# The first chunk's output product in seven half-size products, with its weights' sums a slot earlier

## The chip, the cores and the metric

The kernel runs on one core of one Trainium2 chip. The metric is the device time of one launch in microseconds, the median of three runs. The profile is one execution of the same program, with the engines' instructions, their waits and the transfers recorded: PE is TensorE, DVE VectorE, ACT ScalarE, POOL GpSimd, SP SyncE, which here only starts transfers.

## What is computed

Two layers stand behind one another. The first is an attention over channels, the second a gated feed-forward layer on its result:

```python
qn = q / (norm(q, axis=1) + 1e-6)          # q, k, v: 4 x 6016 x 256
kn = k / (norm(k, axis=1) + 1e-6)
a = softmax(kn.transpose(0, 2, 1) @ qn / tau)   # 256 x 256 for each batch entry
x = (v @ a).reshape(24064, 256)
gate = sigmoid(x @ w_gate)                 # w_gate, w_val: 256 x 1536
out = (gate * (x @ w_val)) @ w_out         # w_out: 1536 x 256
```

The kernel never forms x. It multiplies the 256 x 256 attention weights of a batch entry into w_gate and w_val once, which gives G and H, and then feeds v to these.

## The kernel before

**Tiling.** A batch entry b has 6016 rows, that is 47 tiles of 128. They are worked on in 12 chunks `(b, ci)` of four tiles (512 rows), the last one of three. The hidden width of 1536 is cut into 12 blocks of 128, f = 0 to 11. One pass of the innermost loop, for one f of one chunk, is called a slot here, and slots of a batch entry are counted as 12 ci + f: slot 10 is f = 10 of the first chunk, slot 12 is f = 0 of the second.

**A slot.** `glu(b, ci, f)` runs two matmuls of 128 x 512 into `ps_gate` (weights `gh_G`), ScalarE takes their tanh into `g_sb` (L647), then PE gets what the caller has put in between, then two matmuls of 128 x 512 into `ps_val` (weights `gh_H`), and VectorE joins the two into block f of `hT` (L650). `ps_gate` and `ps_val` have two PSUM buffers each, so the gate matmuls of slot n wait for the tanh of slot n - 2, and the val matmuls of slot n wait for the VectorE instruction of slot n - 2.

**What stands in between.** The output product of chunk n is worked off during chunk n + 1: `out_work` makes a list of matmuls, and `run_work` takes a twelfth of it between the gate and the val matmuls of each slot. Before the change there are two forms of this list:

- The first chunk, `(0, 0)`, is `plain`: for each of its four row tiles 12 matmuls of 128 x 256 (`single`, L754), 48 in all, four in a slot. Each reads a block of `hT` as its stationary operand and a row block of `w_out_sb`. ScalarE copies each finished tile to `out_sb` (L760).
- Every other chunk takes its tiles in two pairs p = 0, 1, and the product of a pair as a 2 x 2 block product (rows by hidden blocks by output columns) in seven half-size products instead of eight: `PRODUCTS` names them, `ORDER` gives their order. Each consists of six matmuls of 128 x 128, so there are 84 matmuls, seven in a slot. The operands are blocks of `hT` and of `w_out_sb`, or sums of such blocks. The sums of `hT` blocks are made on VectorE by `a_sum` (L676, L678, L680: three instructions for the first half of the hidden blocks, at f = 7, 9, 11 of the chunk itself, and three for the second half, at f = 0, 2, 4 of the next chunk). The sums of `w_out` blocks, `w_sums`, are made once. When z1 is done, ScalarE copies three of the four regions to `m_sb` and GpSimd adds in it twice (`part`); when v2 is done, ScalarE copies the PSUM bank to `out_sb` and GpSimd adds twice (`whole`).

**The weights' sums.** `w_out` comes as three float32 tiles `w_f32[0..2]`, each with the rows of four hidden blocks. GpSimd casts them into `w_out_sb` (`copy_w_out`, slot 8), and makes five sums m = 0 to 4, each in three instructions, one for each tile (`sum_w_out`, L228), at the slots 11 (m = 1), 13 (m = 0), 15 (m = 3), 17 (m = 2) and 19 (m = 4). The last one needs the other sign, so there each instruction is followed by a multiplication by -1, on GpSimd too (L230). The products use them as follows: y1 takes sum 1, x1 sum 0, z1 sum 3, z2 sum 2, v2 sum 4; x2 and y2 take `w_out_sb` itself.

**What sets the order.** The order of the instructions on each engine is written out by hand: `side_work` hangs other work on slots, and within a slot the loop first calls `glu`, then puts `a_sum`, then the work hung on that slot. No scheduler moves anything. GpSimd's queue also issues most loads: `load_qk` of the next batch entry at slot 9 (four transfers), `load_v` at slot 10 of the first chunk and at the first slot of the following ones.

The lines of one slot in the main loop that the change touches, with the two tables it uses:

```python
NEXT_SLOTS = {0: 0, 2: 1, 4: 2}
OWN_SLOTS = {7: 0, 9: 1, 11: 2}
...
                    if f in next_sums and prev != (0, 0):
                        a_sum(*prev, 1, next_sums[f])
                if f in OWN_SLOTS and not final and (b, ci) != (0, 0):
                    a_sum(b, ci, 0, OWN_SLOTS[f])
                for fn, a in spill.get((b, ci, f), []) + side.get((ci, f), []):
                    fn(*a)
```

Of the kernel before, what the change touches and what calls it, by code (L numbers as in the profile page):

```python
# [12 lines left out]
ACT = mybir.ActivationFunctionType  # L13
ALU = mybir.AluOpType
# [37 lines left out]
OWN_SLOTS = {7: 0, 9: 1, 11: 2}  # L52
# [3 lines left out]
def kernel(  # L56
# [20 lines left out]
    nc = tc.nc  # L77
# [10 lines left out]
    FC = DFF // P  # L88
# [41 lines left out]
    def mm(out, lhsT, rhs, start, stop, **kw):  # L130
        nc.tensor.matmul(out, lhsT=lhsT, rhs=rhs, start=start, stop=stop, **kw)  # L131
# [30 lines left out]
    t0, nt = groups0[0]  # L162
# [39 lines left out]
    for f0, nf in pieces:  # L202
        if f0 + nf == DFF:
            load_v(0, 1)
        for w, src in enumerate((moe_w_gate, moe_w_val)):
            nc.gpsimd.dma_start(
                out=w_sb[w][f0 // FG][:, :, ds(f0 % FG, nf)],
                in_=src.rearrange("(t p) f -> p t f", p=P)[:, :, ds(f0, nf)],
# [5 lines left out]
    for n in range(FC // TPC):  # L214
        w_f32[n] = f32pool.tile([P, TPC, C], FP32, tag="f32", name="w_f32")
        nc.gpsimd.dma_start(
            out=w_f32[n], in_=moe_w_out.rearrange("(t p) c -> p t c", p=P)[:, n * TPC : (n + 1) * TPC, :]
# [5 lines left out]
    def sum_w_out(m, n):  # L223
        (k0, c0), op, (k1, c1) = B_SUMS[m]
        w = w_f32[n]
        out = w_sums[:, m, n * 2 : (n + 1) * 2, :]
        in0, in1 = w[:, k0::2, ds(c0 * P, P)], w[:, k1::2, ds(c1 * P, P)]
        nc.gpsimd.tensor_tensor(out=out, in0=in0, in1=in1, op=op)  # L228
        if m == 4:
            nc.gpsimd.tensor_scalar(out=out, in0=out, scalar1=-1.0, scalar2=None, op0=ALU.mult)  # L230


    st = {}
# [449 lines left out]
    stores = []  # L683

    def out_tile(b, ci):
        if (b, ci) not in ffn:
            ffn[b, ci] = opool.tile([P, TPC, C], FP32, tag="osb", name="out_sb")
        return ffn[b, ci]

    def out_work(b, ci):  # L690

        nt = groups[ci][1]
        half = nt // 2
        hT = hts[b, ci]
        work = []
        states = [{} for _ in range(half)]
        singles = {}
        plain = (b, ci) == (0, 0)

        def product(p, name, i):  # L700
            state = states[p]
            region, a, w = PRODUCTS[name]
            first = name == "y1" and i == 0
            if first:
                state["ps"] = pso.tile([P, CH], FP32, tag="o", name="ps_o")
            g, j = divmod(i, FC // 4)
            if isinstance(a, tuple):
                lhsT = hT[:, 2 * i + a[1], ds((a[0] * half + p) * P, P)]
            else:
                lhsT = sums[b, ci, g][:, a, j, ds(p * P, P)]  # L710
            rhs = w_out_sb[:, 2 * i + w[0], ds(w[1] * P, P)] if isinstance(w, tuple) else w_sums[:, w, i, :]
            mm(
                state["ps"][:, ds(region * P, P)],
                lhsT,
                rhs,
                start=first,
                stop=(i == FC // 2 - 1),
                skip_group_check=True,
            )
            if i == FC // 2 - 1:  # L720
                if name == "z1":
                    part(p)
                elif name == "v2":
                    whole(p)

        def part(p):

            m = states[p]["m"] = mpool.tile([P, 3, P], FP32, tag="m", name="m_sb")
            nc.scalar.copy(m, states[p]["ps"][:, : 3 * P].rearrange("p (n c) -> p n c", c=P))  # L729
            nc.gpsimd.tensor_tensor(out=m[:, 1, :], in0=m[:, 1, :], in1=m[:, 2, :], op=ALU.add)  # L730
            nc.gpsimd.tensor_tensor(out=m[:, 2, :], in0=m[:, 1, :], in1=m[:, 0, :], op=ALU.add)  # L731

        def whole(p):

            o = out_tile(b, ci)
            nc.scalar.copy(  # L736
                o[:, p : p + half + 1 : half, :],
                states[p]["ps"].rearrange("p (t c) -> p t c", c=C),
            )
            blocks = o.rearrange("p t (h c) -> p (t h) c", c=P)  # L740
            c00, c11 = 2 * p, 2 * (half + p) + 1
            ends = blocks[:, c00 : c11 + 1 : c11 - c00, :]
            mids = blocks[:, c00 + 1 : c11 : max(1, c11 - c00 - 2), :]
            last = (b, ci) == (B - 1, NCH - 2)
            add = nc.gpsimd.tensor_tensor
            add(out=ends, in0=ends, in1=states[p]["m"][:, 1:3, :], op=ALU.add)  # L746
            add(out=ends, in0=ends, in1=mids, op=ALU.subtract)  # L747
            if last:
                t0 = groups[ci][0]
                nc.sync.dma_start(out=out_rows[b][:, t0 + p : t0 + nt : half, :], in_=o[:, p:nt:half, :])  # L750
            elif p == half - 1:
                stores.append((b, ci))

        def single(s, f):  # L754
            if f == 0:
                singles[s] = pso.tile([P, CH], FP32, tag="o", name="ps_o")
            ps = singles[s]
            mm(ps[:, :C], hT[:, f, ds(s * P, P)], w_out_sb[:, f, :], f == 0, f == FC - 1)
            if f == FC - 1:
                nc.scalar.copy(out_tile(b, ci)[:, s, :], ps[:, :C])  # L760
                if plain and s == nt - 1:
                    stores.append((b, ci))

        if plain:
            return [(2, single, t, f) for t in range(nt) for f in range(FC)]
        for p, name in LAST_ORDER if (b, ci) == (B - 1, NCH - 2) else ORDER:
            if p < half:
                for i in range(FC // 2):
                    work.append((1, product, p, name, i))
                if nt % 2 and name == "z1":  # L770
                    for f in range(FC):
                        work.append((2, single, nt - 1, f))
        return work

    def run_work(work, share):

        upto = sum(w[0] for w in work) * share
        done = 0
        while work and done < upto:
            cost, fn, *args = work.pop(0)  # L780
            fn(*args)
            done += cost

    def store():
        while stores:
            b, ci = stores.pop(0)
            t0, nt = groups[ci]
            nc.sync.dma_start(out=out_rows[b][:, t0 : t0 + nt, :], in_=ffn.pop((b, ci))[:, :nt, :])
# [111 lines left out]
    def side_work(b):  # L900
# [4 lines left out]
        def at(slot, fn, *a):  # L905
            side.setdefault(divmod(slot, FC), []).append((fn, a))

        for ci in range(NCH):
            nb, nci = (b, ci + 1) if ci + 1 < NCH else (b + 1, 0)
            lb, lci = (b, ci + 2) if ci + 2 < NCH else (b + 1, ci + 2 - NCH)  # L910
            if nb < B:
                at(ci * FC + 2, transpose_v, nb, nci)
            if lb < B:
                at(ci * FC + (10 if (b, ci) == (0, 0) else 0), load_v, lb, lci)
            if (b, ci) == (0, 0):
                for i in range(FC // TPC):
                    at(8, copy_w_out, i)
                for n, m in enumerate((1, 0, 3, 2, 4)):
                    for i in range(FC // TPC):
                        at(11 + 2 * n, sum_w_out, m, i)  # L920
        n = b + 1
        if n == B:
            return side
# [66 lines left out]
        for i, piece in enumerate(gh_order):  # L990
            slot = GH_SLOTS[i]
# [12 lines left out]
    def gh_pieces(ns):  # L1004
        for n in ns:
            gh(0, gh_first[n], *gh_banks[n % 4])

    prev = None
    for b in range(B):
        side = side_work(b)  # L1010
        for ci in range(NCH):
            final = (b, ci) == (B - 1, NCH - 1)
            for f in range(FC):
                mid = gh_mid.get(f) if (b, ci) == (0, 0) else None
                if prev is not None:
                    mid = lambda: run_work(work, 1 / max(1, FC - final - f))
                elif mid is not None:
                    mid = lambda ns=mid: gh_pieces(ns)
                glu(b, ci, f, mid)
                if prev is not None:  # L1020
                    if f == 4:
                        store()
                    next_sums = LAST_SLOTS if final else NEXT_SLOTS
                    if f in next_sums and prev != (0, 0):
                        a_sum(*prev, 1, next_sums[f])
                if f in OWN_SLOTS and not final and (b, ci) != (0, 0):
                    a_sum(b, ci, 0, OWN_SLOTS[f])
                for fn, a in spill.get((b, ci, f), []) + side.get((ci, f), []):
                    fn(*a)
                if (b, ci) == (0, 0):  # L1030
                    gh_pieces(gh_end.get(f, ()))
            prev = (b, ci)
            if not final:
                work = out_work(*prev)
# [39 lines left out]
```

## Time and profile before

| | |
|---|---|
| time, median of 3 runs | 800.76 us (800.63 to 801.05) |
| span of the profiled execution | 798.3 us, mean granted TensorE clock 0.998 |
| first gate matmul of chunk (0, 0) | 36.66 us |
| first gate matmul of chunk (0, 1) | 51.50 us |
| first slot of chunk (0, 1): output matmuls, then val matmuls, start at | 51.93 and 52.37 us |
| first gate matmul of chunk (0, 2) | 67.21 us |
| the 15 sums on GpSimd (L228) | 52.3 to 70.2 us, 719 to 1372 ns each |
| the three sign changes on GpSimd (L230) | 1102 to 1240 ns each |

Times of the trace count from the start of the span. A line of the timeline gives the start, the time taken by a run of like instructions, the engine, the line of the kernel, the operation with the tiles it writes and reads, how many there are, and in brackets how long the engine stood idle before it and what released it. The ends of matmuls are modelled, so that neighbours overlap a little: the step from one start to the next is the better measure. Most matmuls have the line of the helper `mm`, L131, and are told apart by their tiles.

### The profile page before, as it was taken

To read this page: it belongs to the slowest core of one execution; us is meant where nothing else is said; L and a number is where in the kernel's file an instruction comes from. 1 tells how busy PE (TensorE), PEld (TensorE's weight loads), DVE (VectorE), ACT (ScalarE), POOL (GpSimd) and SP (SyncE) were. 2 spreads that over 40 slices of the span, in tenths; PEclk is the share of its full clock that TensorE was granted. 3 is DMA by queue.
4 is the path that set the end of the run, shared out by engine and by line. 5 is a ranking of instruction groups with operands and counts; after the bars stand their busy time and mean duration, and the time that the engine had idled before them with its cause. 6 is when DMAs were issued, how large, how long until landed. Compare 5 with 4: busy or idle time off the path is not lost.

```text
span 798.3 us, 18307 instructions
## 1 busy us (share of the span) xinstructions
PE 777.6 (97%) x6946; PEld 497.7 (62%) x6946; DVE 695.1 (87%) x1078; ACT 514.0 (64%) x893; POOL 431.1 (54%) x651
## 2 busy tenths in 40 slices
PE   3899999999999999999999999999999999999997
PEld 2556666666666666666666666666666666666666
DVE  5779999999889999998889999899897888888885
ACT  3767677766676766766667777675666555565563
POOL 3568666538643666555844566654753244344333
PEclk9999999999999999999999999999999999999999
DMA  9998868632784898752597598866224223323302
GB/s 214 204 195 144 163 118 178 118 67 53 144 144 90 159 181 152 125 101 53 110 146 117 111 176 158 153 119 106 59 58 93 60 55 89 71 55 86 67 28 73
DMA packets 86744, 91.69 MB, mean 115 GB/s; under 512 B 52864, under 2 KB 58752, under 8 KB 86656
## 3 DMA queue, kind: packets, MB, share of 16 engines
q0 software_dynamic: 29584, 52.38, 38.8%
q1 hardware_dynamic: 56496, 37.30, 20.7%
q8 instruction: 54, 0.88, 0.5%
q10 hardware_dynamic: 576, 0.85, 0.4%
q14 instruction: 34, 0.28, 0.1%
HBM read 79.04 MB, written 24.64 MB: 130 GB/s over the span
## 4 chain that ended last, share of the span: by engine, by line
PE 95%; DMA 4%; DVE 0%; issue 0%; ACT 0%; POOL 0%; DVEq 0%; POOLq 0%
PE ps_gate L131 31%; PE ps_val L131 31%; PE ps_o L131 28%; DMA qk_sb<-in_k_dram 4%; PE ps_s L131 4%; PE ps_gh L131 3%; PE ps_end L131 0%; DVE x_sb L510 0%; PE ps_n L131 0%; PE ps_r L131 0%; ACT e_sb L528 0%; POOL qk_sb L146 0%; DVE x_sb L522 0%; DVE end L810 0%; DVE r L493 0%
## 5 line engine op out<-in xcount | busy, mean ns | idle before, releaser
L647 ACT ACTIVATE g_sb<-ps_gate 128x512 f32<-128x512 f32 (+1 forms) x576 | 338.7, 588 | 244.8 <-PE ps_gate L131 233.3
L650 DVE SCALAR_TENSOR_TENSOR hT<-g_sb,ps_val 128x512 bf16<-128x512 f32 (+1 forms) x576 | 386.6, 671 | 83.0 <-PE ps_val L131 60.2
L131 PE MATMUL ps_gate<-vT,gh_G 128*128 128x512 bf16 (+1 forms) x1152 | 337.6, 375 | 0.0
L131 PE MATMUL ps_val<-vT,gh_H 128*128 128x512 bf16 (+1 forms) x1152 | 337.5, 375 | 0.0
L131 PEld LDWEIGHTS <-sums 128*128 128x128 bf16 x2670 | 183.0, 98 | 82.0
L746 POOL TENSOR_TENSOR out_sb<-out_sb,m_sb 128x256 f32<-128x256 f32 x89 | 70.6, 794 | 189.7 <-ACT out_sb L736 162.2
L131 PE MATMUL ps_o<-w_sums,sums 128*128 128x128 bf16 x1602 | 154.0, 219 | 0.0
L131 PEld LDWEIGHTS <-gh_G 128*128 128x128 bf16 x1152 | 100.8, 98 | 73.5 <-DVE gh_G L596 0.3
L131 PEld LDWEIGHTS <-hT 128*128 128x128 bf16 x1200 | 88.3, 98 | 46.6
L730 POOL TENSOR_TENSOR m_sb<-m_sb 128x128 f32<-128x128 f32 x89 | 50.3, 565 | 118.2 <-ACT m_sb L729 118.0
L747 POOL TENSOR_TENSOR out_sb<-out_sb 128x256 f32<-128x256 f32 x89 | 93.2, 1047 | 7.0
L131 PE MATMUL ps_o<-w_out_sb,sums 128*128 128x128 bf16 x1068 | 96.2, 219 | 0.0
L680 DVE TENSOR_TENSOR sums<-hT 128x1536 bf16<-128x1536 bf16 (+1 forms) x92 | 95.6, 1039 | 0.0
L131 PE MATMUL ps_o<-w_sums,hT 128*128 128x128 bf16 x1068 | 95.4, 219 | 0.0
L131 PEld LDWEIGHTS <-gh_H 128*128 128x128 bf16 x1152 | 90.1, 98 | 3.3 <-DVE gh_H L596 0.3
L678 DVE TENSOR_TENSOR sums<-hT 128x1536 bf16<-128x1536 bf16 (+1 forms) x92 | 86.2, 937 | 0.0
L293 ACT ACTIVATE sq<-qk_sb 128x1024 bf16<-128x1024 bf16 (+1 forms) x61 | 63.1, 1035 | 0.0
L131 PEld LDWEIGHTS <-qs 128*128 128x128 bf16 x348 | 33.8, 98 | 40.3
L731 POOL TENSOR_TENSOR m_sb<-m_sb 128x128 f32<-128x128 f32 x89 | 49.5, 556 | 7.0
L736 ACT COPY out_sb<-ps_o 128x512 f32<-128x512 f32 x89 | 51.8, 582 | 0.0
L676 DVE TENSOR_TENSOR sums<-hT 128x768 bf16<-128x768 bf16 (+1 forms) x92 | 51.6, 561 | 0.0
L131 PEld LDWEIGHTS <-qk_sb 128*128 128x128 bf16 x241 | 25.1, 104 | 38.0 <-issue 10.2
(102 smaller groups left out, 576.6 us busy)
## 6 DMA issues: line engine op xcount, KB each, us to landing
out_dram<-out_sb SPq DMA_DIRECT2D x43, 512.0 KB, 3.4
acc<-sq POOLq DMA_DIRECT2D x45, 256.0 KB, 5.0
v_sb<-in_v_dram POOLq DMA_DIRECT2D x44, 256.0 KB, 5.4
qk_sb<-in_q_dram POOLq DMA_DIRECT2D x35, 256.0 KB, 7.9
qk_sb<-in_k_dram POOLq DMA_DIRECT2D x35, 256.0 KB, 5.8
qk_sb<-in_q_dram POOLq DMA_DIRECT2D x4, 512.0 KB, 11.3
qk_sb<-in_k_dram POOLq DMA_DIRECT2D x4, 512.0 KB, 13.3
w_f<-in_moe_w_out_dram POOLq DMA_DIRECT2D x3, 512.0 KB, 10.0
```

Of the source, the lines that this page charges most:

```text
L131: nc.tensor.matmul(out, lhsT=lhsT, rhs=rhs, start=start, stop=stop, **kw)
L293: nc.scalar.activation(out=s["sq", w, i], in_=qk[b, t0][:, w, u0 : u0 + n, :], func=ACT.Square)
L647: nc.scalar.activation(out=g_sb[:, :n], in_=ps_gate[:, :n], func=ACT.Tanh, scale=0.5)
L650: nc.vector.scalar_tensor_tensor(out=hts[b, ci][:, f, :n], in0=g_sb[:, :n], scalar=1.0, in1=ps_val[:, :n], op0=ALU.add, op1=ALU.mult,)
L676: nc.vector.tensor_tensor(out=out[:, :, 0], in0=x[:, :, 0, 0], in1=x[:, :, 1, 1], op=ALU.add)
L678: nc.vector.tensor_tensor(out=out, in0=x[:, :, 0], in1=x[:, :, 1], op=ALU.add)
L680: nc.vector.tensor_tensor(out=out, in0=x[:, :, :, 0], in1=x[:, :, :, 1], op=ALU.subtract)
L730: nc.gpsimd.tensor_tensor(out=m[:, 1, :], in0=m[:, 1, :], in1=m[:, 2, :], op=ALU.add)
L731: nc.gpsimd.tensor_tensor(out=m[:, 2, :], in0=m[:, 1, :], in1=m[:, 0, :], op=ALU.add)
L736: nc.scalar.copy(o[:, p : p + half + 1 : half, :], states[p]["ps"].rearrange("p (t c) -> p t c", c=C),)
L746: add(out=ends, in0=ends, in1=states[p]["m"][:, 1:3, :], op=ALU.add)
L747: add(out=ends, in0=ends, in1=mids, op=ALU.subtract)
```

## The change

The plain form goes, so that the first chunk's output product is done like all the others: 84 matmuls of 128 x 128 in place of 48 of 128 x 256, with six `a_sum` instructions on VectorE, and with the copies and additions of `part` and `whole`. As the products then need the weights' sums during the second chunk and not only from the third on, the sums are hung on earlier slots: 10, 11, 13, 14, 16 in place of 11, 13, 15, 17, 19. The sign of sum 4 is turned on ScalarE. The purpose is to give PE fewer columns to stream in the second chunk.

```diff
         nc.gpsimd.tensor_tensor(out=out, in0=in0, in1=in1, op=op)
         if m == 4:
-            nc.gpsimd.tensor_scalar(out=out, in0=out, scalar1=-1.0, scalar2=None, op0=ALU.mult)
+            nc.scalar.activation(out=out, in_=out, func=ACT.Copy, scale=-1.0)
...
-        plain = (b, ci) == (0, 0)
...
                 nc.scalar.copy(out_tile(b, ci)[:, s, :], ps[:, :C])
-                if plain and s == nt - 1:
-                    stores.append((b, ci))
-
-        if plain:
-            return [(2, single, t, f) for t in range(nt) for f in range(FC)]
...
-                for n, m in enumerate((1, 0, 3, 2, 4)):
+                for slot, m in ((10, 1), (11, 0), (13, 3), (14, 2), (16, 4)):
                     for i in range(FC // TPC):
-                        at(11 + 2 * n, sum_w_out, m, i)
+                        at(slot, sum_w_out, m, i)
...
-                    if f in next_sums and prev != (0, 0):
+                    if f in next_sums:
                         a_sum(*prev, 1, next_sums[f])
-                if f in OWN_SLOTS and not final and (b, ci) != (0, 0):
+                if f in OWN_SLOTS and not final:
                     a_sum(b, ci, 0, OWN_SLOTS[f])
```

## The prediction

> **What bounds the kernel now.** I read the page's first line, then the waits of PE, then PE's timeline around the second chunk, and last GpSimd's.
>
> ```profile
> PE 777.6 (97%) x6946; PEld 497.7 (62%) x6946; DVE 695.1 (87%) x1078; ACT 514.0 (64%) x893; POOL 431.1 (54%) x651
> PE ps_s L131 <- DMA qk_sb<-in_k_dram: 9.1, 6, 3.1
> PE ps_s L131 <- ACT qk_sb L193: 6.5, 1, 6.5
> PE ps_r L131 <- ACT e_sb L528: 0.7, 1, 0.7
> ```
>
> PE is busy for 97% of the span, and the view of its waits has three rows, all from before the first chunk (16.3 us). From 36.66 us on PE waits for nobody: a microsecond of PE work removed is a microsecond won, and a microsecond in which PE has to wait is one lost, as no later wait exists that could swallow it.
>
> ```profile
> 51.50 0.59 PE L131 MATMUL ps_gate<-vT,gh_G 128*128 128x512 bf16 x2
> 51.93 0.60 PE L131 MATMUL ps_o<-w_out_sb,hT 128*128 128x256 bf16 x4
> 52.37 0.59 PE L131 MATMUL ps_val<-vT,gh_H 128*128 128x512 bf16 x2
> ...
> 67.64 0.55 PE L131 MATMUL ps_o<-w_sums,hT 128*128 128x128 bf16 x7
> 68.03 0.59 PE L131 MATMUL ps_val<-vT,gh_H 128*128 128x512 bf16 x2
> ```
>
> Four plain matmuls take 52.37 - 51.93 = 0.44 us of a slot, seven half-size ones 68.03 - 67.64 = 0.39 us (56 ns each).
>
> ```profile
> 49.63 1.13 POOL L146 DMA_DIRECT2D qk_sb<-in_k_dram  x2
> 50.73 1.09 POOL L146 DMA_DIRECT2D qk_sb<-in_q_dram  x2
> 51.78 0.57 POOL L158 DMA_DIRECT2D v_sb<-in_v_dram  x1
> 52.32 2.13 POOL L228 TENSOR_TENSOR w_sums<-w_f 128x256 bf16<-128x256 f32 x3
> 54.36 0.58 POOL L158 DMA_DIRECT2D v_sb<-in_v_dram  x1
> 54.95 4.16 POOL L228 TENSOR_TENSOR w_sums<-w_f 128x256 bf16<-128x256 f32 x6
> ```
>
> This is the part that decides. GpSimd has no gap here: the transfers of slot 9 and 10 keep it until 52.32, and only then comes the first weights' sum, 4.16 / 6 = 0.69 us each. A new reader of those sums, on PE at 51.93, is earlier than the first of them.
>
> **What the Trainium skill says.** TensorE: Matmul & The Clock Gate (Part 2, Step-by-step) lets weight loads be pulled ahead, while matmuls stay in program order: a half-size product that waits holds up everything behind it. The same page (Architectural detail) calls ScalarE a strict FIFO. Its sustained 81 ns for a matmul of 128 columns with its weights (Back-to-back issue gap) isn't what this trace shows: 56 ns. SBUF — State Buffer (Who interferes with whom) says that a VectorE instruction with two SBUF inputs contends with a GpSimd instruction that reads SBUF. The trace agrees:
>
> ```profile
> 66.20 1.35 POOL L228 TENSOR_TENSOR w_sums<-w_f 128x256 bf16<-128x256 f32 x1
> ...
> 66.01 0.95 DVE L678 TENSOR_TENSOR sums<-hT 128x1536 bf16<-128x1536 bf16 x1
> ```
>
> A sum beside an `a_sum` took 1.35 us in place of 0.69. From 61.2 to 70.2 six sums took 3.65 + 1.35 + 1.37 = 6.37 us in place of 4.14, with seven such VectorE instructions about: some 0.32 us per VectorE instruction on average, 0.66 at most.
>
> **Part by part.**
>
> *Matmuls.* 12 slots lose 0.44 - 0.39 = 0.045 us each: -0.54 us. This is all that the change can win, 0.07%.
>
> *First wait: sum 1.* In the built program the queue of GpSimd is unchanged up to the first sum: slot 10 in place of 11 moves it past no transfer that cost time (the load of slot 10 still stands ahead). Its three parts end near 53.05, 53.75 and 54.47. The first slot of the second chunk has y1 of pair 0 (six matmuls, two for each part of the sum) and one matmul of y1 of pair 1. The last two of y1 wait for 54.47 and a semaphore, I say 54.55; three more steps of 56 ns, and the val matmuls start at 54.72. Unhindered they would start at 51.93 + 0.39 = 52.32. Cost 2.4 us.
>
> *Second wait: sum 3.* Behind sum 1 GpSimd has sum 0 (three, to 56.43), the v load (0.59, to 57.02) and sum 3 (57.71, 58.40, 59.09). Sum 0 is in time for x1, in the second and third slot. z1 begins in the third slot and needs the second part of sum 3 there: 58.50 with its semaphore, val matmuls at 58.56. With the first wait alone they would be there at 54.72 + 2 x 1.257 = 57.23 (a slot is four 0.217 us matmuls and 0.39). Cost 1.33 us. The last part, needed a slot later, is in time.
>
> *Third wait: the sign on ScalarE.* The three sign turns stand on ScalarE's queue between the tanh of f = 4 and that of f = 5, each waiting for a part of sum 4. On GpSimd, sum 2 comes first (to 61.16), then two `m_sb` additions (0.53 each, to 62.2), then sum 4 (to 64.27). The turn has no row in this trace; the page ScalarE: Activation LUTs (What ACT_TABLE_LOAD costs) gives 186 ns + 0.833 ns per column, an estimate of 0.40 us for 256; the nearest rows are 0.37 us (L760, 128x256) and 0.47 us (L594). The tanh of f = 5 so begins near 64.65 and ends near 65.25. Behind it wait the gate matmuls of f = 7, which need its PSUM buffer, and these would be due at 58.56 + 0.43 + 4 x 1.257 = 64.02. Cost 1.28 us.
>
> *Contention.* The new `a_sum` instructions (559, 959, 1073 ns by their rows) fall into this stretch: the last of the first half near 52.9, the second half after f = 0, 2 and 4, and the existing L325 behind. Five VectorE instructions beside GpSimd's chain, at 0.32 us: 1.6 us; between 0 (GpSimd wins each time) and 5 x 0.66 = 3.3. I take 1.6, as the order of starts is open.
>
> *VectorE itself.* Six additions of 5.2 us. VectorE's queue in the second chunk is then 12 x 0.6 for `hT`, 2 x 2.3 of `a_sum` and 4 x 0.72 of L325, L333 and L338: 14.7 us against a chunk of 12 x 1.257 = 15.1 us, lengthened by the waits. At the end of the first chunk its lag is covered by the first wait. Cost 0, up to 0.65 if L333 is stretched again as at 61.48 (1.75 us).
>
> *At no cost.* The additions of `part` and `whole`, 2 x 3 us on GpSimd, come behind the sums there, and the copies on ScalarE (0.47 and 0.58 us) replace L760's; only the first pair of additions lies in a chain above, and is counted. The store moves by nothing that ends last.
>
> Sum: -0.54 + 2.40 + 1.33 + 1.28 + 1.6 = +6.07 us, so 800.76 + 6.07 = 806.8 us.
>
> **The rivals.**
> 1. *Only the first two waits count.* The third is avoided if GpSimd gets to sum 4 sooner than I say. Against it: GpSimd's work between is fixed, with no idle time. -0.54 + 2.40 + 1.33 = +3.2: 804.0 us.
> 2. *Only the first.* The second goes if the two waits overlap more than I count. -0.54 + 2.40 = +1.9: 802.6 us.
> 3. *VectorE becomes the bound as well.* For it: 87% busy, 14.7 of 15.1 us. Against it: the waits give it time. With full contention (3.3) and 0.65: -0.54 + 5.01 + 3.3 + 0.65 = +8.4: 809.2 us.
> 4. *No wait shows, the gain is whole.* For it: the chunk would be 0.54 us shorter. It needs sum 1 by 52.2 us, two microseconds before GpSimd had it. 800.2 us, not slower.
>
> **How the numbers follow.** The forecast gets 0.68, rival 1 0.12, rival 2 0.06, rival 3 0.10, rival 4 0.04. Range: from a little under rival 1, 803.6, to just under rival 3, 809.0; what lies outside is rivals 2 and 4 and most of 3, near 2 in 10. Rival 4 is within 0.2% (1.6 us); rival 2, +1.9, is just over it. So 0.92 slower, 0.06 the same, and 0.02 faster, for a gain that no part of the sum offers.
>
> **What would show it.** PE's waits after: new rows `ps_o` on POOL `w_sums`, near 2.4 + 1.3 us and more by contention, and `ps_gate` on ACT `g_sb` of 1 to 3 us; the first val matmuls of the second chunk near 54.7; ScalarE idle for `w_sums` before f = 5; GpSimd's first sum still at 52.32; the third chunk's first gate matmuls near 73 in place of 67.21. Wrong it would be if PE had no such rows, if the first sum began before 52, or if the gap closed again later in the span.

## The result, and the profile after

The changed kernel takes 808.98 us (median of 6 runs), beside 801.01 us of the kernel before in the same runs: a ratio of 1.0104, 95% interval 1.0091 to 1.0117. It is slower by some 8 us; the forecast was 6 us slower. 809.0 was the upper end of its range, and 800.76 x 1.0104 = 809.1 us lies just above it.

The page's row of PE, and then the view of PE's waits (in total, how often, the longest):

```profile
PE 780.9 (97%) x6968; PEld 499.4 (62%) x6982; DVE 700.7 (87%) x1084; ACT 515.1 (64%) x896; POOL 429.6 (53%) x656
PE ps_s L131 <- DMA qk_sb<-in_k_dram: 7.1, 5, 2.1
PE ps_s L131 <- ACT qk_sb L193: 6.8, 1, 6.8
PE ps_o L131 <- POOL w_sums L228: 3.1, 5, 1.1
PE ps_gate L131 <- ACT g_sb L647: 2.9, 1, 2.9
...
```

The share of busy time on the page says nothing: 97% before and after. The waits say it: two new rows in the stretch of the chunks, for the sums on GpSimd and for the tanh on ScalarE. PE's timeline in the second chunk shows where they lie:

```profile
52.05 0.59 PE L131 MATMUL ps_gate<-vT,gh_G 128*128 128x512 bf16 x2
53.19 0.27 PE L131 MATMUL ps_o<-w_sums,hT 128*128 128x128 bf16 x2 [0.54 <-POOL w_sums L228]
53.88 0.27 PE L131 MATMUL ps_o<-w_sums,hT 128*128 128x128 bf16 x2 [0.41 <-POOL w_sums L228]
55.27 0.33 PE L131 MATMUL ps_o<-w_sums,hT 128*128 128x128 bf16 x3 [1.12 <-POOL w_sums L228]
55.44 0.59 PE L131 MATMUL ps_val<-vT,gh_H 128*128 128x512 bf16 x2
...
58.61 0.27 PE L131 MATMUL ps_o<-w_sums,sums 128*128 128x128 bf16 x2 [0.67 <-POOL w_sums L228]
59.28 0.22 PE L131 MATMUL ps_o<-w_sums,sums 128*128 128x128 bf16 x1 [0.40 <-POOL w_sums L228]
59.34 0.59 PE L131 MATMUL ps_val<-vT,gh_H 128*128 128x512 bf16 x2
...
64.35 0.59 PE L131 MATMUL ps_val<-vT,gh_H 128*128 128x512 bf16 x2
67.81 1.01 PE L131 MATMUL ps_gate<-vT,gh_G 128*128 128x512 bf16 x2 [2.87 <-ACT g_sb L647]
68.62 0.95 PE L131 MATMUL ps_o<-w_sums,sums 128*128 128x128 bf16 x7
69.37 1.06 PE L131 MATMUL ps_val<-vT,gh_H 128*128 128x512 bf16 x2
```

y1 waits three times for the parts of sum 1, z1 twice for those of sum 3, then the gate matmuls of f = 7 wait for the tanh of f = 5. The last two lines show something else. The seven products take 69.37 - 68.62 = 0.75 us where seven take 0.39 elsewhere (56.69 - 56.30, the second slot of this chunk), so PE is running at half speed. The windows view gives the granted clock as the last number but two (after the busy times of PE, its weight loads, VectorE, ScalarE and GpSimd):

```profile
64.40:67.80 3.40, 0.54 (x5) 0.14 (x2) 1.17 (x3) 1.77 (x5) 3.40 (x5) 0.99 0.06 11
67.80:71.20 3.40, 3.39 (x15) 1.71 (x15) 2.67 (x5) 2.26 (x4) 2.42 (x5) 0.51 0.94 143
```

In the stretch after the wait the clock was 0.51 (cut exactly at 67.72 and 71.13 us, it is 0.50 for 3.41 us). GpSimd, the source of all this, is busy without a gap:

```profile
51.76 0.58 POOL L158 DMA_DIRECT2D v_sb<-in_v_dram  x1
52.30 4.97 POOL L228 TENSOR_TENSOR w_sums<-w_f 128x256 bf16<-128x256 f32 x6
57.22 0.57 POOL L158 DMA_DIRECT2D v_sb<-in_v_dram  x1
57.81 4.86 POOL L228 TENSOR_TENSOR w_sums<-w_f 128x256 bf16<-128x256 f32 x6
62.64 0.45 POOL L729 TENSOR_TENSOR m_sb<-m_sb 128x128 f32<-128x128 f32 x1
63.16 0.45 POOL L730 TENSOR_TENSOR m_sb<-m_sb 128x128 f32<-128x128 f32 x1
63.58 3.25 POOL L228 TENSOR_TENSOR w_sums<-w_f 128x256 bf16<-128x256 f32 x3
```

The first sum starts at 52.30, as before at 52.32, in spite of its earlier slot. ScalarE's three sign turns stand behind the last of these:

```profile
62.21 0.60 ACT L647 ACTIVATE g_sb<-ps_gate 128x512 f32<-128x512 f32 x1
65.05 0.42 ACT L230 ACTIVATE w_sums<-w_sums 128x256 bf16<-128x256 bf16 x1 [2.24 <-POOL w_sums L228]
66.18 0.42 ACT L230 ACTIVATE w_sums<-w_sums 128x256 bf16<-128x256 bf16 x1 [0.71 <-POOL w_sums L228]
66.86 0.42 ACT L230 ACTIVATE w_sums<-w_sums 128x256 bf16<-128x256 bf16 x1 [0.27 <-POOL w_sums L228]
67.18 0.58 ACT L647 ACTIVATE g_sb<-ps_gate 128x512 f32<-128x512 f32 x1
```

**Where 8.6 us of the span went** (798.3 to 806.9), by the start of the same matmuls in the two timelines:

| matmuls | before | after | later by | added here |
|---|---|---|---|---|
| val in the first chunk, before anything differs on PE | 48.46 | 48.71 | 0.25 | 0.25 |
| val, f = 0 of chunk 2 | 52.37 | 55.44 | 3.07 | 2.82 |
| val, f = 2 | 54.97 | 59.34 | 4.37 | 1.30 |
| gate, f = 7 | 60.60 | 67.81 | 7.21 | 2.84 |
| first gate of chunk 3 | 67.21 | 75.81 | 8.60 | 1.39 |

Of the 2.82 us, 0.30 passed before the first wait, where VectorE was late with the first chunk (the first gate matmuls of the second chunk start at 52.05 in place of 51.50); as GpSimd sets when the first wait ends, they cost nothing of their own. From the third chunk on nothing is added or won back. The last row has no wait in it: it is the half clock (3.69 us from the gate matmuls at 67.81 to the val matmuls of f = 8 at 71.50, where four groups of 0.43 or 0.39 us and one more of 0.43 make 2.07: 1.6 us) less the shorter slots.

### The profile page after: what moved, and what is told of

Its sections match the earlier page's. It is cut to its first block, busy times and chain, and to the rows that moved or that the text cites. A ratio compares the mean times of both kernels' runs of the same rounds, so it can differ in the third digit from the quotient of the medians.

```text
span 806.9 us, 18381 instructions
## 1 busy us (share of the span) xinstructions
PE 780.9 (97%) x6968; PEld 499.4 (62%) x6982; DVE 700.7 (87%) x1084; ACT 515.1 (64%) x896; POOL 429.6 (53%) x656
## 4 chain that ended last, share of the span: by engine, by line
PE 91%; DMA 4%; POOL 3%; issue 0%; ACT 0%; DVE 0%; POOLq 0%; ACTq 0%
PE ps_gate L131 29%; PE ps_val L131 29%; PE ps_o L131 27%; PE ps_s L131 3%; DMA qk_sb<-in_k_dram 3%; PE ps_gh L131 2%; POOL w_sums L228 2%; DMA w_f<-in_moe_w_out_dram 1%; POOL qk_sb L146 0%; POOL w_gate L206 0%; POOL w_val L206 0%; ACT sq L254 0%; POOL v_sb L158 0%; POOL w_out_sb L221 0%; PE ps_end L131 0%
## 5 line engine op out<-in xcount | busy, mean ns | idle before, releaser
L650 DVE SCALAR_TENSOR_TENSOR hT<-g_sb,ps_val 128x512 bf16<-128x512 f32 (+1 forms) x576 | 386.0, 671 | 85.8 <-PE ps_val L131 62.1
L131 PEld LDWEIGHTS <-sums 128*128 128x128 bf16 x2730 | 187.6, 98 | 85.3 <-issue 1.9
L131 PE MATMUL ps_o<-w_sums,sums 128*128 128x128 bf16 x1638 | 158.1, 219 | 1.1 <-POOL w_sums L228 1.1
L131 PEld LDWEIGHTS <-hT 128*128 128x128 bf16 x1176 | 85.4, 98 | 47.0 <-issue 1.4
L746 POOL TENSOR_TENSOR out_sb<-out_sb 128x256 f32<-128x256 f32 x91 | 96.2, 1057 | 7.1
L131 PE MATMUL ps_o<-w_sums,hT 128*128 128x128 bf16 x1092 | 97.8, 219 | 2.1 <-POOL w_sums L228 2.1
L131 PE MATMUL ps_o<-w_out_sb,sums 128*128 128x128 bf16 x1092 | 98.3, 219 | 0.0
L680 DVE TENSOR_TENSOR sums<-hT 128x1536 bf16<-128x1536 bf16 (+1 forms) x94 | 97.7, 1040 | 0.0
L678 DVE TENSOR_TENSOR sums<-hT 128x1536 bf16<-128x1536 bf16 (+1 forms) x94 | 88.8, 944 | 0.0
L676 DVE TENSOR_TENSOR sums<-hT 128x768 bf16<-128x768 bf16 (+1 forms) x94 | 53.2, 566 | 0.0
```

Source lines behind the costliest of these rows:

```text
L650: nc.vector.scalar_tensor_tensor(out=hts[b, ci][:, f, :n], in0=g_sb[:, :n], scalar=1.0, in1=ps_val[:, :n], op0=ALU.add, op1=ALU.mult,)
L676: nc.vector.tensor_tensor(out=out[:, :, 0], in0=x[:, :, 0, 0], in1=x[:, :, 1, 1], op=ALU.add)
L678: nc.vector.tensor_tensor(out=out, in0=x[:, :, 0], in1=x[:, :, 1], op=ALU.add)
L680: nc.vector.tensor_tensor(out=out, in0=x[:, :, :, 0], in1=x[:, :, :, 1], op=ALU.subtract)
```

## The experiments

Each ran beside the kernel before on the same chip; the median of before was 800.70 to 801.04 us in them. A ratio is that of the run to the kernel before.

**E1: the sign turns two slots later.** The three turns move into a function of their own, hung on slot 18.

```diff
-        if m == 4:
-            nc.scalar.activation(out=out, in_=out, func=ACT.Copy, scale=-1.0)
+    def turn_sign(n):
+        out = w_sums[:, 4, n * 2 : (n + 1) * 2, :]
+        nc.scalar.activation(out=out, in_=out, func=ACT.Copy, scale=-1.0)
...
+                for i in range(FC // TPC):
+                    at(18, turn_sign, i)
```

> The changed kernel with the three sign turns hung two slots later on ScalarE's queue, behind the tanh of f = 6. Theory of the waits: the tanh of f = 5 no longer waits for sum 4, so the 2.9 us wait of ps_gate on g_sb goes, and with it the 3.4 us at half clock (1.7 us); what is left is up to 1 us of the tanh of f = 7 or of v2 waiting for the last turns. Expected 804.0 to 805.5 us, PE waits for w_sums still 3 to 4 us. If VectorE's six additions were the cost, the time stays within 1 us of 809.

Measured: 806.46 us, ratio 1.0070 (1.0055 to 1.0085). The wait on g_sb is gone, and 2.5 us with it, less than the 3.5 to 5 expected. PE's timeline shows why:

```profile
55.96 0.33 PE L131 MATMUL ps_o<-w_sums,hT 128*128 128x128 bf16 x3 [1.12 <-POOL w_sums L228]
56.63 1.06 PE L131 MATMUL ps_gate<-vT,gh_G 128*128 128x512 bf16 x2
59.08 1.00 PE L131 MATMUL ps_gate<-vT,gh_G 128*128 128x512 bf16 x2
60.74 0.59 PE L131 MATMUL ps_gate<-vT,gh_G 128*128 128x512 bf16 x2
...
67.60 0.59 PE L131 MATMUL ps_val<-vT,gh_H 128*128 128x512 bf16 x2 [0.86 <-DVE hT L652]
```

(L652 is the changed kernel's L650; the edit adds two lines.) The half clock came all the same, now after the first wait: a gate pair takes 1.06 us in place of 0.59 from 56.63 on. It covered the wait for sum 3, which has no row here, and moved it into slow matmuls. Behind, PE waited 0.86 us for VectorE.

**E2: the first chunk's products read other weights.**

```diff
+            if (b, ci) == (0, 0) and not isinstance(w, tuple):
+                w = (0, 0)
             rhs = w_out_sb[:, 2 * i + w[0], ds(w[1] * P, P)] if isinstance(w, tuple) else w_sums[:, w, i, :]
```

> In the first chunk alone every product that should read a weights' sum reads a block of w_out_sb instead, so its results are other numbers; the sums, their sign turn and all of VectorE's and GpSimd's work stay. If the three waits are terms that add, the first two (some 4.1 us) are saved: 804.9 us. If they are stations on one GpSimd chain that runs on its own time, PE comes to the third station earlier and waits there longer (6 to 7 us in place of 2.9), and the time stays at 808 to 809.5.

Measured: 809.23 us, ratio 1.0106 (1.0090 to 1.0121), the same as the changed kernel. The waits for w_sums are gone, and one wait took their place:

```profile
59.50 0.59 PE L131 MATMUL ps_gate<-vT,gh_G 128*128 128x512 bf16 x2
67.19 1.01 PE L131 MATMUL ps_gate<-vT,gh_G 128*128 128x512 bf16 x2 [6.27 <-ACT g_sb L647]
```

The gate matmuls of f = 7 start at 67.19, against 67.81 in the changed kernel. So the three waits aren't three costs that can be taken off one by one. They are stations on one GpSimd chain, and the last station sets the time: with it in place, the first two cost 0.6 us. Even these are not won, for another reason: the half clock lasts twice as long here, from 66.14 to 72.97 us, and the third chunk's first gate matmuls start at 76.38, after 75.81 in the changed kernel. The longer idle stretch of PE has its price in the clock.

**E3: PE kept busy over the third wait.**

```diff
+                if (b, ci, f) == (0, 1, 7):
+                    ps = pss.tile([P, CH], FP32, tag="s", name="ps_fill")
+                    for _ in range(13):
+                        mm(ps, ones_bf, ones_wide, True, True)
                 glu(b, ci, f, mid)
```

> The changed kernel with 13 matmuls of 128x512 on constants (2.8 us, results unused) put in front of the gate matmuls of f = 7 in the second chunk, where PE stood idle for 2.9 us. If the half clock of 67.8 to 71.2 us is a consequence of that idle time, it goes, and the added work costs nothing: 1.7 us faster than the changed kernel, 807.3. If the clock fell for another reason, or the wait isn't idle PE time, the time is 809 or, with the added work exposed, up to 812.

Measured: 807.81 us, ratio 1.0082 (1.0065 to 1.0098). The intervals of this run and of the changed kernel overlap a little, so the trace has to say it:

```profile
66.42 2.75 PE L131 MATMUL ps_fill<-ones_wide,ones_bf 128*128 128x512 bf16 x12
69.24 0.59 PE L131 MATMUL ps_gate<-vT,gh_G 128*128 128x512 bf16 x2
70.49 0.59 PE L131 MATMUL ps_gate<-vT,gh_G 128*128 128x512 bf16 x2
...
75.61 0.59 PE L131 MATMUL ps_gate<-vT,gh_G 128*128 128x512 bf16 x2
```

From the gate matmuls of f = 7 to the third chunk's it is 75.61 - 69.24 = 6.37 us, against 75.81 - 67.81 = 8.00: 1.63 us less, with 2.8 us of matmuls more. They cost nothing, as the tanh of f = 5 ended only at 69.2. This execution had reached the second chunk 1.42 us later than the changed kernel's (first gate matmuls at 53.47 and 52.05), by waits at the start, so its span is only 0.2 us shorter; the medians differ by 1.2 us. The half clock is a consequence of the idle PE.

**E4: the schedule of the sums and the sign alone, with the first chunk plain.** In the kernel before:

```diff
-            nc.gpsimd.tensor_scalar(out=out, in0=out, scalar1=-1.0, scalar2=None, op0=ALU.mult)
+            nc.scalar.activation(out=out, in_=out, func=ACT.Copy, scale=-1.0)
...
-                for n, m in enumerate((1, 0, 3, 2, 4)):
+                for slot, m in ((10, 1), (11, 0), (13, 3), (14, 2), (16, 4)):
```

> The kernel before (first chunk plain), with only the earlier slots of the sums and the sign turn on ScalarE. No product of the first chunk reads a sum. Theory of the waits: GpSimd's chain ends sum 4 near 63 to 64 us, the tanh of f = 5 waits for it, gate matmuls of f = 7 start near 64.5 in place of 60.6: some 4 us and 1.7 us of half clock, 805.5 to 807. If the cost is in the seven products and their a_sum, this is 800.8, as before.

Measured: 806.25 us, ratio 1.0066 (1.0051 to 1.0081), with no product in this chunk that reads a sum:

```profile
64.52 1.01 PE L131 MATMUL ps_gate<-vT,gh_G 128*128 128x512 bf16 x2 [3.46 <-ACT g_sb L647]
```

PE waits for the tanh for 3.46 us and runs at half clock behind it. The sign turn, meant to relieve GpSimd, costs two thirds of the loss (5.5 of 8.0 us) together with the earlier slots; neither was tried without the other.

**E5: both ways to wait for a sum taken out.** E2, with the turns as in E1 but at slot 24.

> As e2 (products of the first chunk read w_out_sb blocks in place of the sums, so they are other numbers), and the sign turns are hung on the first slot of the third chunk, long after sum 4 is made and before anything reads it. No PE instruction waits for GpSimd's sums then, by either way; the seven products, the six a_sum, the copies and the additions are all there. Theory of the waits: 800.3 to 801.0 us, no half clock after the start. If VectorE's additions or their contention carry part of the loss by themselves, 802 to 804.

Measured: 802.39 us, ratio 1.0009 (0.9993 to 1.0025): 6.6 us of the loss are gone. By the interval what is left can't be told from the kernel before, but all 12 runs lie above the median of before in this series, 800.93, and the medians differ by 1.5 us. The trace fits that: PE waits for `hT` three times, 0.84, 0.28 and 0.87 us. VectorE comes late as soon as PE doesn't, the second of the two readings in the expectation.

**E6: the sign back on GpSimd.**

```diff
-            nc.scalar.activation(out=out, in_=out, func=ACT.Copy, scale=-1.0)
+            nc.gpsimd.tensor_scalar(out=out, in0=out, scalar1=-1.0, scalar2=None, op0=ALU.mult)
```

> The changed kernel with the sign turned on GpSimd again, as before. Theory of one GpSimd chain: it only becomes longer (three turns of 1.1 us more), PE waits for the signed sum 4 in v2 instead of for the tanh, some 3 us in several pieces; 806.5 to 809. If the place on ScalarE's queue is the fault by itself, the wait goes: 804 to 805.5.

Measured: 809.19 us, ratio 1.0104 (1.0085 to 1.0123), no better. v2 now waits for L230 (0.93 us), z1 for an `a_sum` that came late (1.15 us), and the half clock came after the first wait as in E1.

**E7: the six a_sum alone, in the kernel before.**

```diff
-                    if f in next_sums and prev != (0, 0):
+                    if f in next_sums:
...
-                if f in OWN_SLOTS and not final and (b, ci) != (0, 0):
+                if f in OWN_SLOTS and not final:
```

> The kernel before with the six a_sum of the first chunk added on VectorE, their results unused. Theory of the waits: at most a short wait of ps_val on hT near 51 us (0.3 us), 800.8 to 801.3; GpSimd's first six sums take near 5.0 us in place of 4.2, but nobody waits. If VectorE is the bound of these two chunks: 803 or more.

Measured: 803.04 us, ratio 1.0025 (1.0016 to 1.0033): 2.1 us, which I had not expected. PE waits for `hT` for 0.59, 0.84 and 0.47 us. Two instructions of the timelines of VectorE and GpSimd show the reason:

```profile
57.50 2.95 DVE L678 TENSOR_TENSOR sums<-hT 128x1536 bf16<-128x1536 bf16 x1
...
56.16 4.87 POOL L228 TENSOR_TENSOR w_sums<-w_f 128x256 bf16<-128x256 f32 x6
```

L678 took 2.95 us beside a run of GpSimd sums, in place of 0.95. The first of the three waits came before any sum: there L676 took 1.17 us, in place of 0.55, beside GpSimd's last cast of `w_out`.

**E8 and E9: the sums in time.** E9 against the changed kernel (E8 also has both loads at slot 3):

```diff
+                    for m in (1, 0, 3):
+                        at(8 if m != 3 or i < 2 else 10, sum_w_out, m, i)
+                    at(12, copy_w_out, i)
+                for m in (2, 4):
...
+                        at(13, sum_w_out, m, i)
+                for i in range(FC // TPC):
+                    at(18, turn_sign, i)
...
+                own = {8: 0, 10: 1, 11: 2} if (b, ci) == (0, 0) else OWN_SLOTS
```

> The changed kernel in an order in which the sums come in time: sums 1, 0 and 3 on GpSimd as soon as each tile of w_out lands (slot 8), the casts behind them at slot 12, sums 2 and 4 at 13, the sign on ScalarE at slot 18, the loads of slots 9 and 10 at slot 3, where GpSimd is idle, and the first chunk's a_sum at f = 8, 10, 11. Theory of the waits: PE waits neither for w_sums nor for g_sb, the third chunk begins 0.3 to 0.6 us earlier than before, 800.0 to 800.9 us. If the seven products cost more than they save, 801.5 or more.

Measured: 808.73 us, ratio 1.0093 (1.0079 to 1.0107). The expected 800 to 801 us were missed by far. No wait for a sum is left, but the first gate matmuls of the second chunk waited 4.29 us for `vT`, the transposing transfer of its rows, which now met the loads moved to slot 3: it landed 15.6 us after its issue, against 8.4 in the kernel before and 8.0 in E9, where these loads are back in their places. The half clock followed, for 6.83 us. It tells nothing of the sums.

> As e8, but the loads of slots 9 and 10 stay at these slots, behind the first eight sums, so that the transposing transfer of the second chunk's rows has the queues to itself as before. PE should wait neither for the transfer nor for w_sums nor for g_sb. Theory now, after e7: VectorE's six a_sum beside GpSimd's sums are a second cost of 1 to 2 us that the waits only hid, so 801.0 to 802.5 us, PE's waits being on hT. If the lateness of the sums were the whole cost: 800.0 to 800.7.

Measured: 805.82 us, ratio 1.0060 (1.0046 to 1.0074). This is above the expected range too. PE waits neither for `vT` nor for a sum nor for the tanh, and is still late, by `a_sum`: 2.21 us at 58.63, and a half clock behind it. VectorE's and GpSimd's timelines:

```profile
55.04 3.53 DVE L678 TENSOR_TENSOR sums<-hT 128x768 bf16<-128x768 bf16 x1
59.69 3.86 DVE L680 TENSOR_TENSOR sums<-hT 128x1536 bf16<-128x1536 bf16 x1
...
55.06 3.00 POOL L221 CAST w_out_sb<-w_f 128x1024 bf16<-128x1024 f32 x3
58.60 4.13 POOL L228 TENSOR_TENSOR w_sums<-w_f 128x256 bf16<-128x256 f32 x6
```

(L678 and L680 are the changed kernel's L676 and L678; the edit adds two lines.) An addition of 0.55 us took 3.53, beside three casts at their full pace of 1.0 us; the next, of 0.95 us, took 3.86 beside six sums at their full pace of 0.69. VectorE waited over several GpSimd instructions in a row, not for one of them: over the three casts, and over the last four of the six sums.

**E10: E7 without GpSimd's sums.**

```diff
+    def fill_sums():
+        nc.gpsimd.memset(w_sums, 0.01)
...
+                at(7, fill_sums)
...
-                        at(11 + 2 * n, sum_w_out, m, i)
```

> As e7 (the kernel before with the six a_sum of the first chunk added, unused), and GpSimd makes no weights' sums: w_sums is filled with a constant while GpSimd waits for w_out, so all later products are other numbers. If e7's loss of 2.1 us is VectorE's own work, the waits of ps_val on hT stay near 1.9 us: 802.5 to 803. If it is contention with GpSimd's sums, L678 falls from up to 2.95 us to 0.95, the waits shrink to 0.5 us or less, and the time is 800.9 to 801.5.

Measured: 801.19 us, ratio 1.0000 (0.9988 to 1.0011). The six a_sum take 0.55 and 0.95 us each, and PE's view of waits has no row on `hT`. So the 2.1 us of E7 were contention with GpSimd, all but the 0.5 us by which the medians still differ, and within that VectorE's own work is free. (The casts of `w_out` also ended before the first a_sum here, so the run doesn't part the sums from the cast.)

**E11: the changed kernel without GpSimd's sums.** The same edit to the changed kernel.

> The changed kernel without the weights' sums and their sign turns on GpSimd and ScalarE: w_sums is filled with a constant while GpSimd waits for w_out, so all products that use it are other numbers. The seven products, the six a_sum, the copies and additions of the first chunk are all there. If the whole loss comes from the sums' chain (waits for it, half clock, VectorE held up by it), 800.0 to 800.7 us, the third chunk beginning 0.5 us earlier than before relative to the second. If any of the loss belongs to the seven products themselves, 801.2 or more.

Measured: 801.83 us, ratio 1.0018 (1.0002 to 1.0035). That is above 801.2, where the expectation blamed the seven products, but the trace doesn't: the slots are 1.25 us in place of 1.30, which is the gain of 0.5 us that the change is for. It is given back to short waits for `hT` (0.19 and 0.48 us) and to 0.84 us for `vT` of the third chunk. Before the longer wait for `hT`, L325 took 1.28 us in place of 0.69 (E10) beside the additions of `part`, which the change brings along: GpSimd holds VectorE up without the sums too. The wait for `vT` has no row in the changed kernel. The transfer landed 9.7 us after its issue here, with the next loads issued beside it (58.40 to 60.57 us), and 4.0 us in the changed kernel, where GpSimd came to these loads only at 66.78; that the loads are the cause was not tested.

## Why the prediction was right in its mechanism and short in its size

- *No slack on PE, so that any wait is lost for good*: right; the gap of 8.60 us at the third chunk is the 8.6 us of the span.
- *Matmuls, -0.54 us*: right in its step (1.253 us in the changed kernel's undisturbed slots, as (64.35 - 60.59) / 3 from the val matmuls of f = 3 to those of f = 6), and seen in E11's slots.
- *First wait, 2.4 us*: measured 2.82 in the table. Its starting point, GpSimd's first sum at 52.3 in spite of the earlier slot, held to 0.02 us. What it lacks is contention: the last part of sum 1 came at 55.2 and not 54.5, 0.7 us, of which the later start of the first chunk hides 0.25 in the table.
- *Second wait, 1.33 us*: 1.30.
- *Third wait, 1.28 us plus its share of contention (three of five instructions, 0.96)*: 2.84, short by 0.6. The mechanism was right, the tanh of f = 5 behind the sign turns; the mis-sized term is contention. GpSimd's 15 sums took 4.97 + 4.86 + 3.25 = 13.08 us, where 15 x 0.693 make 10.4: 2.7 us, not the 1.6 of the sum. Three of them took 1.43 or 1.44 us and one 1.17, so that the 0.66 us that the prediction had as the most was the rule where a sum was held up, not its average of 0.32.
- *What failed is a term that the sum did not have.* It priced a wait of PE at its length. PE's clock falls to half behind an idle stretch, which cost another 1.6 us (E3 takes it away by keeping PE busy). The clock stood at 0.9 or more throughout in the page before, and I took it as given. But each slice of that page is 20 us long. The windows view of the same trace shows the half clock, behind a stretch in which PE was busy for 0.64 us of 3.41:

```profile
16.65:20.06 3.41, 0.64 (x6) 0.42 (x5) 3.34 (x6) 0.79 (x1) 1.06 (x2) 1.00 1.06 213
20.06:23.48 3.42, 3.12 (x15) 2.16 (x15) 2.36 (x5) 2.01 (x2) 0.00 (x0) 0.50 1.05 212
```

  TensorE: Matmul & The Clock Gate (Part 1, What's actually happening) describes this: the clock is halved after an idle window of some 3.4 us, and given back after one busy window. The trace agrees in the length, 3.41 us at 0.50. It differs on the idle window: PE was still busy for 0.64 us of the 3.41 before the fall (64.30 to 67.72), and in E1 for 1.33.
- *Both misses were needed to leave the range.* Contention 1.1 us short makes 807.9, the half clock alone 808.4, both below 809.0; together they make 809.5.
- *VectorE at no cost, up to 0.65*: right for the changed kernel, where the waits give it time, and wrong as a statement on the additions. E7 puts them at 2.1 us where PE doesn't wait, and nearly all of that is contention (E10). The prediction took contention as a cost of GpSimd, apart from one stretched L333; E7 and E9 show VectorE as the one that is held up.
- *The waits add up*: true as an account of the time that passed, wrong as a guide to what to mend. E2 takes two of them out, and PE comes to the third only 0.6 us earlier.
- *The rivals*: the one with a VectorE bound (809.2) came nearest in number. Its full contention (3.3) is nearer to the measured 2.7 than the forecast's 1.6, but its own mechanism isn't there: the changed kernel has no row of PE waiting for `hT`, and the half clock that made up the number is in no rival.

No version here beats the kernel before. The shorter slots, 12 x 0.045 us, bound what there is to win at about 0.5 us, less than these measurements tell from nothing.

## What to carry to other kernels

An earlier place in a queue is earlier only if the engine is free there: look at what stands before it in the engine's timeline, and compare that with the time of the first reader. An instruction that waits on an in-order queue is paid by whatever stands behind it, so a small job moved to another engine can cost more than it saves (E4). Price the waits on one chain by the last of them, not by their sum. And price a stall of PE at its length and, where PE was idle for some 2 us or more of one 3.41 us window, at half of the next window besides (1.6 us in the changed kernel); several short waits in one window count together.

## What the runs showed of the hardware

- The clock falls and comes back on a fixed beat. In each of the twelve traces that show more than one stretch at half clock, all their beginnings lie a whole number of 3.413 us apart: in the changed kernel the stretches are 26.76 to 30.17 and 67.72 to 71.13 us, with 11 such windows between them. What the traces let one count is how long PE was busy in the window before a fall. The same three waits of the first slot (0.54, 0.41 and 1.12 us) lie in two windows of the changed kernel and in one of E1 (windows view; PE's busy time comes first behind the length, the clock last but two):

```profile
50.65:54.06 3.41, 2.34 (x12) 1.08 (x12) 3.41 (x6) 1.79 (x3) 3.41 (x7) 1.00 0.95 144
54.06:57.48 3.42, 2.30 (x20) 1.34 (x18) 1.93 (x3) 0.60 (x1) 3.42 (x5) 1.00 1.12 211
...
53.06:56.47 3.41, 1.33 (x11) 0.66 (x10) 2.27 (x4) 0.65 (x2) 3.41 (x4) 1.00 1.11 207
56.47:59.88 3.41, 3.41 (x15) 1.66 (x13) 2.00 (x3) 0.60 (x1) 3.39 (x7) 0.50 0.90 145
```

  The first two lines are the changed kernel's, and the clock stayed; the last two are E1's, and it fell. Over all traces, as far as the clock is recorded, windows with up to 1.65 us idle kept the clock, those with 1.99 us or more lost it for the next one, and at 1.76 to 1.81 us both happened; the ends of matmuls are modelled, so the bound is rough. The half clock lasts one window where PE works through it, and two in E2 and E8, where PE was busy for 2.36 and 1.56 us of the first. So the same waits can cost 1.6 us more or not, by where they fall on the beat.
- A VectorE addition with both inputs in SBUF, beside GpSimd instructions that follow one another without a gap, was held over three casts (3.53 us for 0.55), four sums (3.86 us for 0.95) and three sums (2.95 us for 0.95), while these kept their pace of 1.0 and 0.69 us. Then it went in and GpSimd waited: the sixth sum of E7's run took 1.43 us. It isn't always so: in the changed kernel the longest such addition took 1.45 us beside sums without a gap. What decides wasn't found. SBUF — State Buffer (Who interferes with whom) names the contention and leaves the loser to the order of issue; that the loser waits over several instructions is what these runs add.
- In E8 a transposing transfer landed 15.6 us after its issue at 42.74 us, with loads of 1.25 MB issued from 40.5 to 46.2 us; with these loads 9 us or more later, in E9, it took 8.0 us.
